# Linear attention, routed experts and a gated MLP on one core: sums and scales of the next expert at the step's end, y stored from ScalarE's queue, raw weights loaded one unit ahead

## The chip, the cores and the metric

One core of one Trainium2 chip runs the kernel. The metric is the device time of one execution in microseconds (us), here the median of three runs. TensorE (PE) does the matmuls, VectorE (DVE), ScalarE (ACT) and GpSimd (POOL) the elementwise work, SyncE (SP) issues most of the DMAs. Each of these engines carries out its own instructions in program order and waits on semaphores for the others.

## What is computed

Three stages follow each other (cut to what matters):

```python
# 1 linear attention, 8 batches x 8 heads x 576 tokens x 64
kv = einsum(softmax(k, over tokens), v);  x = softmax(q) @ kv      # x: 4608 x 512
# 2 routed experts, 8 of them, one per token
e = argmax(normalised(x) @ normalised(expert_emb).T / tau)
x = gate_w * (relu(x @ w1[e]) @ w2[e])                             # 512 -> 1024 -> 512
# 3 gated MLP
xn = x / rms(x) * rms_g
out = (silu(xn @ w_gate) * (xn @ w_val)) @ w_out                   # 512 -> 1536 -> 512
```

## The kernel before, in words

After the attention and the routing (up to about 188 us) the tokens are sorted by expert into blocks of 128, and the expert phase goes over them one block per **step** (`block(b, b0)`, from L1055). With these inputs 37 blocks hold tokens: steps 0 to 17 belong to one expert, 18 to 26 to the next, 27 to 31 and 32 to 36 to two more. All products are made of fp16 pieces: a high and a low half of each fp32 operand, three matmuls for one.

In step b PE runs the first product of block b (`g1_mm`, L1002: 96 matmuls of 128 columns from the transposed tokens `xT` and the weights `w1h`, `w1l`) and then the second product of block b-1 (`g2`, L1019: 24 matmuls of 512 columns from `hh`, `hl` and `w2h`, `w2l`). ACT evacuates the first product to `hh` (L1008) and DVE takes the remainder `hl` (L1009), both in two halves. ACT evacuates the second product of block b-1 to the tile `y` (`g2_ev`, L1026), scaled by a column `scl` that DVE made (L992); POOL writes the token's number into the last column of `y` (L1027) and SP stores the tile to `yscr` (L1028, 256.5 KB).

The weights of the next expert are made ready in the same steps by work that stands in conditional parts (`tc.If`), whose flags `r` and `rz` are read from a table at run time:

- last step of an expert (17, 26, 31): `split_stage(0, ...)` splits `w1` into halves (ACT L954, DVE L959), then SP loads the raw `w1` of the expert after it (`load_stage`, L898);
- first step of an expert (`rz` = 1: 18, 27, 32): `second_split` does the same for `w2` and loads the next (L901);
- third step (`rz` = 2: 2, 20, 29): `norm_parts`, six sums of squares on ACT (L913) and two maxima on DVE (L915) of the raw weights;
- fourth step (`rz` = 3: 3, 21, 30): `norm_scale`, a chain of small DVE instructions from L938 to L141 that makes the scale `wS` and its inverse `wI`.

`second_split`, `norm_parts` and `norm_scale` stand in one conditional part, `If(rz > 0)` at L1086, between the hidden activations and the evacuation of y. The instructions of PE's `g2` wait until ACT and DVE have left this part in the step before, since it can write `w2h` and `w2l`.

Beside this a filler (`fill`, three steps at L1085 and one at the end of the step) prepares the 36 weight tiles of the gated MLP: SP loads a `raw` tile (L1151, 512 KB), DVE turns it from float64 to float32 (L141, L142, L1181 to L1185), and later ACT (L1160) and DVE (L1161) split it. Three `raw` buffers are there and the load of unit k+2 is issued when unit k begins. From the end of step 31 on what is left of the filler is drained.

`prefetch(b)` at the start of a step has POOL gather the tokens of block b+3 and SP issue the transpose DMA of block b+2 into `xT` (L988, three buffers).

All DMAs of SP's and ACT's queues take turns on eight completion counters, DMAHW0 to DMAHW7 in the order listings below. A DMA is not issued before the one that had the counter before it has landed; a conditional part with DMAs in it that is passed over also moves its counters on, and waits in the same way.

From about 597 us the gated MLP runs to the end. Its matmuls follow each other almost without a gap.

Of the kernel before, what the change touches and what calls it, by code (L numbers as in the profile page):

```python
# [9 lines left out]
F32 = mybir.dt.float32  # L10
# [8 lines left out]
ET = mybir.EngineType  # L19
# [4 lines left out]
NT, DM = B * S, H * D  # L24
E, F = 8, 1024
FF = 1536
NTI = NT // 128
NBLK = NTI + E - 1
# [104 lines left out]
class Kern:  # L133
# [441 lines left out]
    def route_ops(self, s):  # L575
# [5 lines left out]
        for g in range(NTI // GT):  # L581
# [64 lines left out]
            for j in range(n):  # L646
                self.bd[i0 + j] = s.op(
                    ("V", 0.16), lambda j=j, i0=i0, bx=bx: self.ts(self.B[:, i0 + j, 0:129].rearrange("p (a c) -> p a c", c=3), self.io3[:, :, 0:3], bx["w"][:, j : j + 1], op0=ALU.is_equal),
                    [w], 0.05 if last else pr + 3, use=[T], late=last)
# [371 lines left out]
        self.yp[b] = p  # L1021

    def g2_ev(self, b):
        nc, p = self.nc, self.yp.pop(b)
        y = self.mp.tile([128, DM + 1], F32, tag="y", name=f"y{b}", bufs=3)
        nc.scalar.activation(y[:, 0:DM], p, AF.Copy, scale=self.scl.pop(b))  # L1026
        nc.gpsimd.tensor_copy(y[:, DM : DM + 1], self.tokf[:, b : b + 1])  # L1027
        nc.sync.dma_start(self.yscr[b * 128 : b * 128 + 128, :], y)  # L1028

    def reg(self, k, b, engines, mx=1):  # L1030
        return self.nc.values_load(self.flag[0:1, k, b : b + 1], engines=engines, min_val=0, max_val=mx)
# [23 lines left out]
    def block(self, b, b0):  # L1055


        tc = self.tc
        es = (ET.Activation, ET.DVE, ET.SP)
        r = self.reg(0, b, es, 4) if b + 1 < NBLK else None  # L1060
        rz = self.reg(1, b, es, 3)
        rx = [self.reg(2, k, (ET.SP,), E - 1) for k in (b, b + 1) if k < NBLK]
        self.h[b] = tuple(self.mp.tile([128, E, 128], F16, tag=t, name=f"{t}{b}", bufs=2) for t in ("hh", "hl"))
        p = [self.g1_mm(b, hf) for hf in range(2)]
        self.xT.pop(b)
        if b > b0:
            self.g2(b - 1)
        self.g1_ev(b, 0, p[0])
        if r is not None:
            with tc.If(r > 0):  # L1070
                with tc.If(r > 1):
                    if b > b0:
                        with tc.If(r > 3):
                            self.second_split(rx[0])
                    with tc.If(r > 2):
                        self.norm_parts()
                    self.norm_scale()
                self.split_stage(0, (0, 1))
        self.g1_ev(b, 1, p[1])
        if r is not None:  # L1080
            with tc.If(r > 0):
                self.split_stage(0, (2, 3))
                self.load_stage(rx[1], ("w1",))
        if b:
            self.fill(FILL[0])  # L1085
        with tc.If(rz > 0):  # L1086
            with tc.If(rz < 2) as c:
                if b > b0:
                    self.second_split(rx[0])
            with c.Else():  # L1090
                with tc.If(rz < 3) as c2:
                    self.norm_parts()
                with c2.Else():
                    self.norm_scale()
        self.scale_of(b)
        if b > b0:
            self.g2_ev(b - 1)
        if b:
            self.fill(FILL[1])

    def last(self, b):
        self.g2(b)
        if b + 1 < NBLK:
            r, rx = self.reg(0, b, (ET.Activation, ET.DVE, ET.SP), 4), self.reg(2, b + 1, (ET.SP,), E - 1)
            with self.tc.If(r > 0):
                self.second_split(rx)
        self.g2_ev(b)
# [4 lines left out]

    def experts(self, b0, b1):
        if b0 == 0:
            self.experts_start()
        for b in range(b0, b1):
            self.prefetch(b)
            self.block(b, 0)
        self.drain(self.filler)

    def tail(self):

        lv = self.reg(3, 0, (ET.PE, ET.Activation, ET.DVE, ET.SP, ET.Pool), NBLK)
        for b0, b1 in TAIL:
            with self.tc.If(lv > b0):
                for b in range(b0, b1):
                    if b > NTI:
                        self.gather(b)
                        self.gather_f(b)
                        self.transp(b)  # L1130
                    self.block(b, b0)
                self.last(b)


    def prep_units(self):

        nc, v, A = self.nc, self.nc.vector, self.A
        p = self.pp
        nc.scalar.dma_start(self.rms, A["rms"].rearrange("(c p) -> p c", p=128))
        order = [(m, u) for m in "gvo" for u in range(12)]  # L1140
        raws = {}

        def load(k):
            if k < len(order):
                m, u = order[k]
                if m == "o":
                    src = A["wo"][u * 128 : u * 128 + 128, :]
                else:
                    src = A["w" + m][(u // 3) * 128 : (u // 3) * 128 + 128, (u % 3) * 512 : (u % 3) * 512 + 512]
                t = p.tile([128, 512], mybir.dt.int64, tag="raw", name=f"raw{k}", bufs=3)  # L1150
                nc.sync.dma_start(t, src)  # L1151
                raws[k] = t

        def f32(k):
            return self.W[:, k + 1].rearrange("p a b -> p (a b)").bitcast(F32)

        def final(m, k0, sc):
            for j in range(12):
                w, c = k0 + j, sc if m == "o" else sc[:, j // 3 : j // 3 + 1]
                nc.scalar.activation(self.W[:, w, 0, :], f32(w), AF.Copy, scale=c)  # L1160
                v.scalar_tensor_tensor(self.W[:, w, 1, :], f32(w), c, self.W[:, w, 0, :], ALU.mult, ALU.subtract)  # L1161
                yield

        load(0)
        load(1)
        fin = iter(())
        yield
        yield from self.slot_steps()
        for k, (m, u) in enumerate(order):
            load(k + 2)  # L1170
            if u == 0:
                mx = p.tile([128, 12], F32, tag="mx", name=f"mx{m}")
            r = raws.pop(k).bitcast(I32).rearrange("p (n t) -> p n t", t=2)
            lo, hi = r[:, :, 0], r[:, :, 1]
            a = p.tile([128, 512], I32, tag="pa", name=f"pa{k}")
            c = p.tile([128, 512], I32, tag="pc", name=f"pc{k}")
            self.ts(a, hi, 0x7FFFFFFF, op0=ALU.bitwise_and)
            self.ts(c, hi, -0x80000000, 0x40000000, ALU.bitwise_and, ALU.bitwise_or)
            self.ts(a.bitcast(F32), a.bitcast(F32), HI_MIN, op0=ALU.max)
            yield  # L1180
            v.scalar_tensor_tensor(c, lo, 29, c, ALU.logical_shift_right, ALU.bitwise_xor)  # L1181
            self.ts(a, a, 3, 0x7FFFFFFF, ALU.logical_shift_left, ALU.bitwise_and)
            yield
            v.tensor_tensor(f32(k).bitcast(I32), a, c, ALU.bitwise_xor)
            v.tensor_reduce(mx[:, u : u + 1], f32(k), axis=AX.X, op=ALU.max, apply_absolute_value=True)  # L1185
            next(fin, None)
            yield
            if u == 11:
                fin = final(m, k - 11, self.w_scale(m, mx))
        for k, _ in enumerate(fin):  # L1190
            yield
            if k % 2:
                yield
# [446 lines left out]
```

## Time and profile before

| | |
|---|---|
| median of 3 runs | 1386.21 us (1385.81, 1386.21, 1386.93) |
| profiled execution | 1388.57 us |
| span of the profile in it | 1386.8 us |
| PE busy | 1337.3 us, 96% |
| DVE, ACT, POOL busy | 843.2, 577.7, 445.7 us |
| expert phase | from about 188 to 597 us |
| mean granted clock of TensorE | 0.985 |

The span is the part of the execution that the profile shows; 1.8 us of the profiled execution lie around it. A row of a timeline gives the start, the length, the engine, the line and operation, the tiles, and in brackets how long the engine had been idle before and what ended that.

### The profile page before, as it was taken

The page shows a single profiled execution, that of the slowest core. Times are in us where ns is not written, and L with a number is a line of the kernel's source. Part 1 is how long each engine was busy: PE and PEld are TensorE (multiplying, and loading weights), DVE is VectorE, ACT ScalarE, POOL GpSimd, SP SyncE. Part 2 cuts the span into 40 slices and gives each one's busy share as a digit, 9 for nine tenths or more (in the row PEclk, how much of TensorE's full clock was granted, in tenths as well). Part 3 has the DMA queues.
Part 4 walks back from the last instruction along what each step waited for, and adds up shares of the span by engine and source line. Part 5 has one row for each costly group of instructions (what it writes and reads, how often), then busy time and mean ns, then how long its engine had stood idle before and what let it go on. Part 6 is the DMA issues. An engine that isn't in the chain of part 4 may idle for free.

```text
span 1386.8 us, 29691 instructions
## 1 busy us (share of the span) xinstructions
PE 1337.3 (96%) x11415; PEld 984.3 (71%) x11415; DVE 843.2 (61%) x1842; ACT 577.7 (42%) x1104; POOL 445.7 (32%) x447
## 2 busy tenths in 40 slices
PE   8999679999998999999999999999999999999998
PEld 8988567777775766744486784867858678586783
DVE  5899877566797776257856363563535536355350
ACT  5888813112334356335543243342423424234231
POOL 4777652222222222043632222322132221322211
PEclk8999889999999999999999999999999999999999
DMA  8799376755596565520211303112031130402100
GB/s 296 268 295 304 109 225 144 147 154 137 136 244 154 161 164 145 133 57 0 70 45 31 84 2 80 35 37 79 2 84 32 41 75 1 91 25 47 39 1 31
DMA packets 151977, 145.78 MB, mean 105 GB/s; under 512 B 108901, under 2 KB 108937, under 8 KB 151761
## 3 DMA queue, kind: packets, MB, share of 16 engines
q1 hardware_dynamic: 141328, 114.64, 31.5%
q0 software_dynamic: 9904, 28.62, 6.9%
q8 instruction: 91, 1.49, 0.5%
q14 instruction: 126, 1.02, 0.3%
q10 hardware_dynamic: 528, 0.00, 0.0%
HBM read 87.35 MB, written 30.45 MB: 85 GB/s over the span
## 4 chain that ended last, share of the span: by engine, by line
PE 46%; DVE 5%; issue 3%; ACT 1%; DMA 1%; POOL 0%; POOLq 0%; DVEq 0%; ACTq 0%
PE po L1466 16%; PE pc L1382 9%; PE pa L1382 9%; PE pd L1382 9%; PE pb L1382 4%; DVE a L1336 1%; DVE xn L1298 1%; DVE ul L1457 1%; DVE hold L1354 1%; DVE u L1455 1%; DMA out<-o,tokr 1%; DVE S L1354 1%; ACT uh L1456 0%; DMA xnT<-xn 0%; POOL ul L1426 0%
## 5 line engine op out<-in xcount | busy, mean ns | idle before, releaser
L1466 PE MATMUL po<-W,uh 128*128 128x512 f16 x864 | 256.9, 379 | 0.0
L1382 PEld LDWEIGHTS <-W 128*128 128x128 f16 x2304 | 225.4, 98 | 28.8 <-issue 0.9
L1002 PE MATMUL hp<-xT,w1h 128*128 128x128 f16 x2368 | 205.4, 220 | 2.7 <-DMA xT<-xg 1.4
L1002 PE MATMUL hp<-xT,w1l 128*128 128x128 f16 x1184 | 203.0, 221 | 4.1 <-DVEq L1070 4.1
L1002 PEld LDWEIGHTS <-w1h 128*128 128x128 f16 x2368 | 185.3, 99 | 11.4 <-ACTq L1070 1.8
L1382 PEld LDWEIGHTS <-S 128*128 128x128 f16 x1728 | 169.1, 98 | 19.6
L1466 PE MATMUL po<-W,ul 128*128 128x512 f16 x432 | 163.7, 379 | 0.0
L1466 PEld LDWEIGHTS <-uh 128*128 128x128 f16 x864 | 84.5, 98 | 100.3
L1382 PE MATMUL pa<-xnT,W 128*128 128x256 f16 x1152 | 141.5, 273 | 0.5 <-ACT s L1391 0.5
L1002 PEld LDWEIGHTS <-w1l 128*128 128x128 f16 x1184 | 116.8, 99 | 4.7 <-DVEq L1070 4.6
L1019 PE MATMUL yp<-w2h,hh 128*128 128x512 f16 x296 | 112.1, 379 | 3.6 <-ACT wjunk L913 3.5
L1019 PE MATMUL yp<-w2l,hh 128*128 128x512 f16 x296 | 112.2, 379 | 2.6 <-DVE wI L141 2.4
L1394 DVE TENSOR_TENSOR u<-pb,s 128x512 f32<-128x512 f32 x48 | 33.2, 691 | 131.4 <-PE pb L1382 109.3
L1019 PEld LDWEIGHTS <-hh 128*128 128x128 f16 x592 | 56.4, 98 | 69.2 <-issue 8.9
L1009 DVE SCALAR_TENSOR_TENSOR hl<-hp,hh 128x512 f16<-128x512 f32 x74 | 51.1, 690 | 85.4 <-ACTq L1070 43.4
L1426 POOL TENSOR_TENSOR ul<-u,uh 128x512 f16<-128x512 f32 x32 | 37.0, 1156 | 184.5 <-ACT uh L1425 184.5
L1425 ACT ACTIVATE uh<-u 128x512 f16<-128x512 f32 x48 | 30.2, 630 | 145.9 <-DVE u L1423 145.9
L1008 ACT ACTIVATE hh<-hp 128x512 f16<-128x512 f32 x74 | 44.0, 595 | 111.9 <-PE hp L1002 102.1
L1471 POOL DMA_INDIRECT out<-o,tokr x36 | 37.1, 1030 | 160.7 <-ACT o L1470 160.6
L1466 PEld LDWEIGHTS <-ul 128*128 128x128 f16 x432 | 42.3, 98 | 51.0
L974 POOL DMA_INDIRECT xf<-fscr,tok x37 | 42.9, 1160 | 89.8 <-DVE scl L992 74.3
L1470 ACT ACTIVATE o<-po,co 128x512 f32<-128x512 f32 x36 | 24.7, 685 | 111.1 <-PE po L1466 111.1
(347 smaller groups left out, 2580.8 us busy)
## 6 DMA issues: line engine op xcount, KB each, us to landing
yscr<-y SPq DMA_DIRECT2D x37, 256.5 KB, 3.3
kt<-in_kT SPq DMA_DIRECT2D x16, 576.0 KB, 6.0
q<-in_q SPq DMA_DIRECT2D x12, 768.0 KB, 6.8
xscr<-row SPq DMA_DIRECT2D x36, 256.0 KB, 3.7
vt<-in_v SPq DMA_DIRECT2D x8, 1024.0 KB, 8.5
w1s<-in_w SPq DMA_DIRECT2D x8, 1024.0 KB, 7.2
w2s<-in_w SPq DMA_DIRECT2D x8, 1024.0 KB, 7.9
raw<-in_wg SPq DMA_DIRECT2D x12, 512.0 KB, 3.7
```

Of the source, the lines that this page charges most:

```text
L974: self.nc.gpsimd.indirect_dma_start(out=out, out_offset=None, in_=src, in_offset=bass.IndirectOffsetOnAxis(ap=self.tok[:, b : b + 1], axis=0),
L1002: nc.tensor.matmul(p[:, fc * 128 : fc * 128 + 128], w[:, dc, fs], xT[:, x, :], start=(fc == 0 and k == 0), stop=(fc == 3 and k == 11), ski ...
L1008: self.nc.scalar.activation(oh, p, AF.Relu)
L1009: self.nc.vector.scalar_tensor_tensor(ol, p, 0.0, oh, ALU.max, ALU.subtract)
L1019: nc.tensor.matmul(p, h[:, fc, :], w[:, fc, :], start=k == 0, stop=k == 23)
L1354: self.nc.vector.tensor_tensor(lo, t, hi, ALU.subtract)
L1382: nc.tensor.matmul(p[:, q * 256 : q * 256 + 256], self.left(k, self.m_, i, q, dcl, w), x[:, r, c : c + 256], start=first and n == 0, stop= ...
L1394: v.tensor_tensor(u2, b, s1, ALU.add)
L1425: nc.scalar.activation(uh[sl], uv, AF.Copy)
L1426: (v if i == 2 else nc.gpsimd).tensor_tensor(ul[sl], uv, uh[sl], ALU.subtract)
L1466: nc.tensor.matmul(p, t[:, fc, sl], self.W[:, 24 + fc, w, :], start=k == 0, stop=k == 35)
L1471: nc.gpsimd.indirect_dma_start(out=self.A["out"], out_offset=bass.IndirectOffsetOnAxis(ap=self.tokr[j][:, s : s + 1], axis=0), in_=o, in_o ...
```

## The change

1. `g2_ev` issues the store of `y` from ACT's queue, right behind ACT's evacuation, and no longer from SP's. The tile is allocated and POOL's copy of the token numbers made at the start of the step (`y_rows`).
2. `norm_parts` and `norm_scale` leave the conditional part ahead of the y evacuation and get one of their own at the step's end, `If(rz > 1)`, behind y and the last filler step. The part ahead keeps `second_split` alone, and is left out in step 0.
3. The load of a raw tile is issued one unit ahead (`load(k + 1)`) in place of two; the load of the second tile ahead of the phase goes.
4. The expert number of the next step is kept in a register (`self.rx`), which saves SP one register load per step.

```diff
     def g2_ev(self, b):
-        nc, p = self.nc, self.yp.pop(b)
-        y = self.mp.tile([128, DM + 1], F32, tag="y", name=f"y{b}", bufs=3)
+        nc, p, y = self.nc, self.yp.pop(b), self.y.pop(b)
         nc.scalar.activation(y[:, 0:DM], p, AF.Copy, scale=self.scl.pop(b))
-        nc.gpsimd.tensor_copy(y[:, DM : DM + 1], self.tokf[:, b : b + 1])
-        nc.sync.dma_start(self.yscr[b * 128 : b * 128 + 128, :], y)
+        nc.scalar.dma_start(self.yscr[b * 128 : b * 128 + 128, :], y)
+
+    def y_rows(self, b):
+        self.y[b] = self.mp.tile([128, DM + 1], F32, tag="y", name=f"y{b}", bufs=3)
+        self.nc.gpsimd.tensor_copy(self.y[b][:, DM : DM + 1], self.tokf[:, b : b + 1])
...
     def block(self, b, b0):
...
-        rx = [self.reg(2, k, (ET.SP,), E - 1) for k in (b, b + 1) if k < NBLK]
+        rx = [self.rx[k] if k in self.rx else self.reg(2, k, (ET.SP,), E - 1) for k in (b, b + 1) if k < NBLK]
+        self.rx = {b + 1: rx[-1]}
+        if b > b0:
+            self.y_rows(b - 1)
...
         if b:
             self.fill(FILL[0])
-        with tc.If(rz > 0):
-            with tc.If(rz < 2) as c:
-                if b > b0:
+        if b > b0:
+            with tc.If(rz > 0):
+                with tc.If(rz < 2):
                     self.second_split(rx[0])
-            with c.Else():
-                with tc.If(rz < 3) as c2:
-                    self.norm_parts()
-                with c2.Else():
-                    self.norm_scale()
         self.scale_of(b)
         if b > b0:
             self.g2_ev(b - 1)
         if b:
             self.fill(FILL[1])
+        with tc.If(rz > 1):
+            with tc.If(rz < 3) as c:
+                self.norm_parts()
+            with c.Else():
+                self.norm_scale()
...
     def prep_units(self):
...
         load(0)
-        load(1)
...
         for k, (m, u) in enumerate(order):
-            load(k + 2)
+            load(k + 1)
```

How the instructions stand, on ACT in step 20 (a step with `norm_parts`), before, from the last filler step to the first `hh` of step 21:

```order
L1160 ACTIVATE W<-W,rscv 128x512
L1086 COMPARE_AND_BRANCH
L1087 COMPARE_AND_BRANCH
L954 ACTIVATE w2h<-w2s,wS 128x1024 x4
L1087 UNCONDITIONAL_BRANCH
L1091 COMPARE_AND_BRANCH
L913 ACTIVATE wjunk,wq<-w1s 128x1024 x4
L913 ACTIVATE wjunk,wq<-w2s 128x1024 x2
L1091 UNCONDITIONAL_BRANCH x2
L1086 UNCONDITIONAL_BRANCH
L1026 ACTIVATE y_9262<-yp_9120,scl_8928 128x512
L1008 ACTIVATE hh_9322<-hp_0_9324 128x512
```

and in the change (y_8836 is the same tile, y of block 19):

```order
L1168 ACTIVATE W<-W,rscv 128x512
L1092 COMPARE_AND_BRANCH
L1093 COMPARE_AND_BRANCH
L954 ACTIVATE w2h<-w2s,wS 128x1024 x4
L1092 UNCONDITIONAL_BRANCH
L1025 ACTIVATE y_8836<-yp_8938,scl_8725 128x512
L1026 DMA yscr<-y_8836 128x513
L1100 COMPARE_AND_BRANCH
L1101 COMPARE_AND_BRANCH
L913 ACTIVATE wjunk,wq<-w1s 128x1024 x4
L913 ACTIVATE wjunk,wq<-w2s 128x1024 x2
L1008 ACTIVATE hh_9131<-hp_0_9133 128x512
```

The six sums (L913) now stand behind the y evacuation and behind ACT's own issue of the store, and ahead of the next `hh`.

On SP, the end of step 19 and the start of step 20, before, with what each waits for (raw_8872 and raw_8958 are units 25 and 26, y_8930 is y of block 18, xT_8974 the transposed tokens of block 22):

```order
L1151 DMA raw_8872<-in_wo 128x512 [waits DMAHW4_49,DVE_49]
L1086 COMPARE_AND_BRANCH
L1087 COMPARE_AND_BRANCH
L1087 UNCONDITIONAL_BRANCH
L1086 UNCONDITIONAL_BRANCH [waits DMAHW5_49,DMAHW6_49]
L1028 DMA yscr<-y_8930 128x513 [waits DMAHW7_49,Activation_49,Pool_49]
L1151 DMA raw_8958<-in_wo 128x512 [waits DMAHW2_49,DMAHW0_49,DVE_49]
L988 DMA_TRANSPOSE xT_8974<-xg_8634 128x8x128 [waits DMAHW1_49,DMASW4_49,PE_49]
```

and in the change (raw_8699 and raw_8753 are units 24 and 25, xT_8800 the tokens of block 22 again), with the store that now stands on ACT as the last row:

```order
L1159 DMA raw_8699<-in_wo 128x512 [waits DMAHW3_49,DVE_49]
L1092 COMPARE_AND_BRANCH
L1093 COMPARE_AND_BRANCH
L1092 UNCONDITIONAL_BRANCH [waits DMAHW4_49,DMAHW5_49]
L1159 DMA raw_8753<-in_wo 128x512 [waits DMAHW6_49,DMAHW1_49,DVE_49]
L988 DMA_TRANSPOSE xT_8800<-xg_8469 128x8x128 [waits DMAHW0_49,DMAHW4_49,DMASW4_49,PE_49]
L1026 DMA yscr<-y_8836 128x513 [waits DMAHW0_49,Activation_49,Pool_49]
```

Ahead of the transpose SP has no y store any more. The store of y of block 19 on ACT uses the counter DMAHW0, which the transpose of block 22 had just before it.

## Rows read from the trace of the kernel before

**Rows 1.** The page's busy time by engine (us, share of span, instructions), PE's part of it.
```profile
PE 1337.3 (96%) x11415; PEld 984.3 (71%) x11415; DVE 843.2 (61%) x1842; ACT 577.7 (42%) x1104; POOL 445.7 (32%) x447
```
**Rows 2.** Windows: stretch, its us, busy us of each engine, clock, DMA share, GB/s.
```profile
400.00:440.00 40.00, 35.29 (x412) 25.87 (x411) 33.05 (x92) 15.90 (x26) 9.02 (x11) 1.00 0.73 171
500.00:550.00 50.00, 46.57 (x531) 33.52 (x529) 33.48 (x82) 28.62 (x42) 7.29 (x9) 1.00 0.52 130
600.00:1387.00 787.00, 779.95 (x5605) 548.10 (x5603) 409.87 (x680) 287.90 (x557) 223.95 (x192) 1.00 0.17 41
```
**Rows 3.** Waits of PE, 180 to 600 us: in total, times, longest.
```profile
PE yp L1019 <- ACT wjunk L913: 3.5, 6, 2.7
PE yp L1019 <- DVE wI L141: 2.4, 2, 1.5
```
**Rows 4.** Timeline of PE, 405 to 440 us, the two longest waits.
```profile
418.89 0.38 PE L1019 MATMUL yp<-w2h,hh 128*128 128x512 f16 x1 [2.70 <-ACT wjunk L913]
...
432.30 0.38 PE L1019 MATMUL yp<-w2l,hh 128*128 128x512 f16 x1 [1.54 <-DVE wI L141]
```
**Rows 5.** Timeline of ACT: the same evacuation in two undisturbed steps one after the other.
```profile
255.51 0.60 ACT L1008 ACTIVATE hh<-hp 128x512 f16<-128x512 f32 x1 [1.69 <-PE hp L1002]
...
266.05 0.60 ACT L1008 ACTIVATE hh<-hp 128x512 f16<-128x512 f32 x1 [2.00 <-PE hp L1002]
```
**Rows 6.** Timeline of ACT, 405 to 428 us: first sum of step 20, and what follows them.
```profile
415.33 1.06 ACT L913 ACTIVATE wjunk<-w1s 128x1024 bf16<-128x1024 f32 x1 [5.80 <-SPq L1081]
...
422.29 0.67 ACT L1026 ACTIVATE y<-yp,scl 128x512 f32<-128x512 f32 x1
422.86 1.30 ACT L1008 ACTIVATE hh<-hp 128x512 f16<-128x512 f32 x2
```
**Rows 7.** Timeline of DVE: unit 25 begins; the scales of step 21, first instruction, and behind them.
```profile
414.60 0.42 DVE L141 TENSOR_SCALAR pa<-raw 128x512 int32<-128x512 int32 x1
...
429.09 0.16 DVE L938 TENSOR_TENSOR wq<-wq 128x2 f32<-128x2 f32 x1
...
432.68 0.16 DVE L992 TENSOR_TENSOR scl<-xf,comp 128x1 f32<-128x1 f32 x1
```
**Rows 8.** Timeline of SP's queue (issues), around steps 19 and 20.
```profile
397.70 3.86 SPq L988 DMA_TRANSPOSE xT<-xg  x1
...
409.16 0.33 SPq L1028 DMA_DIRECT2D yscr<-y  x1
...
410.07 1.26 SPq L988 DMA_TRANSPOSE xT<-xg  x1
```
**Rows 9.** Transpose, us from issue to landing: all 37; those issued at 397.70 and at 410.07.
```profile
DMA to landing us min/median/max: 3.4/5.8/11.4
...
xT<-xg SPq DMA_TRANSPOSE x1, 11.4
...
xT<-xg SPq DMA_TRANSPOSE x1, 7.3
```
**Rows 10.** Raw tile, us from issue to landing, all 36.
```profile
DMA to landing us min/median/max: 3.5/3.7/6.1
```
**Rows 11.** Waits of SP and DVE, 190 to 600 us: in total, times, longest.
```profile
SPq L1028 <- ACT y L1026: 89.0, 23, 8.0
SPq L1028 <- DMA xT<-xg: 3.2, 1, 3.2
DVE scl L992 <- DVEq L1086: 6.2, 25, 0.6
```
**Rows 12.** Timeline: the one DMA of this phase that ACT issues.
```profile
190.78 0.42 ACTq L1139 DMA_DIRECT2D rmsg<-in_rms  x1
```
**Rows 13.** Timeline of PE and ACT at the start of step 33, the last weights' split.
```profile
546.77 0.28 PE L1002 MATMUL hp<-xT,w1h 128*128 128x128 f16 x2 [1.28 <-ACTq L1070]
...
546.07 1.31 ACT L1008 ACTIVATE hh<-hp 128x512 f16<-128x512 f32 x2 [0.44 <-issue]
```
**Rows 14.** Timeline of PE at the end of the phase.
```profile
597.38 2.75 PE L1451 MATMUL pg<-xnT,W 128*128 128x512 f16 x12 [2.47 <-SPq L1105]
```

More of the change, by code (lines that the diff above doesn't have):

```diff
@@ L1099, in block @@
             self.fill(FILL[1])
+        with tc.If(rz > 1):
[3 more added lines that the diff above has]
+                self.norm_scale()
     def last(self, b):
+        self.y_rows(b)
         self.g2(b)
@@ L1114, in experts @@
         if b0 == 0:
+            self.rx, self.y = {}, {}
             self.experts_start()
@@ L1125, in tail @@
             with self.tc.If(lv > b0):
+                self.rx = {}
                 for b in range(b0, b1):
```

## The prediction, made before the change was run

> **What bounds the kernel now.** I read the page first: PE is busy for 1337.3 us, 96% of the span [rows 1], so only PE's idle time can be won. The windows by stretch say where it lies: from 600 us on PE is busy for 779.95 of 787 us and the clock is 1.00, while 400 to 440 us shows 35.29 of 40 and 500 to 550 us 46.57 of 50 [rows 2]. The change touches the expert phase alone, and what comes after 600 us moves as one piece. Then the waits of PE: its second product waits 3.5 us in six places for the sums (`wjunk`) and 2.4 us in two for the scales (`wI`) [rows 3]. This, 5.9 us, is all that moving those two parts can take away. PE's timeline puts most of it into two steps: 2.70 us at 418.89 and 1.54 us at 432.30 [rows 4], with three more of 0.16 us behind the first. I call these B (2.70 + 3 x 0.16 = 3.18) and C (1.54); what is left of the 5.9, about 1.2 us, lies in steps 30 and 31. In undisturbed steps PE waits for nothing: the same evacuation comes at 255.51 and 266.05, ended each time by PE [rows 5], which gives 10.54 us a step.
>
> **Why B is there.** ACT starts the sums of step 20 only at 415.33, after 5.80 us of waiting for SP, whose passage through the conditional parts of step 20 releases them [rows 6]. SP came late: it issued the transpose of block 22 at 410.07, just behind the y store at 409.16 [rows 8]. That store was held by the counter it shares with the transpose before, issued at 397.70, which took 11.4 us to land [rows 8, 9, 11]: 397.70 + 11.4 = 409.1. So the root of B is one slow transpose, and the sums' place only passes it on to PE.
>
> **Part 1, sums and scales at the step's end.** PE's g2 of step 21 wants to start at 418.89 - 2.70 = 416.2. It no longer waits for the sums, so B goes, and C with it: -4.7 us. But the sums are still 7 us of ACT (415.33 to 422.29) and everything queued behind them on ACT is late: `hh` of step 21, then DVE's `hl`, three filler steps, and the conditional part that PE's next g2 waits for. Before, DVE got there 429.09 - 415.33 = 13.8 us after the sums began [rows 6, 7]. Of this 0.6 us was the y evacuation (422.29 to 422.86), which now stands ahead of them; a further conditional part that is passed over costs DVE 6.2 / 25 = 0.25 us [rows 11]. That makes 13.4 us. PE wants that g2 at 416.2 + 10.54 = 426.7. With S the start of the sums, PE waits S + 13.4 - 426.7.
>
> What sets S now? ACT's y evacuation is done near 411.5, but the store behind it is ACT's own, and it shares its counter with the transpose of block 22: ACT stands there until that has landed. SP no longer has y stores ahead of its transposes, but the transpose of block 21 stays behind the `w2` load and comes only about 1 us sooner; raw unit 25 behind it shares its counter, so block 22's is issued near 408.6, some 1.5 us earlier than before. It lands 5.8 us (median) to 7.3 us (what this one took) later [rows 9]: S = 414.6 to 416.1 with 0.2 us for the passage. I take the middle, 415.4: PE waits 415.4 + 13.4 - 426.7 = 2.1 us. The scales (3.6 us of DVE, 429.09 to 432.68 [rows 7]) follow a step later; their wait lies between nothing and C's 1.5 us, and I take 0.3, because PE's own delay moves its need with it. So 2.4 of the 4.7 us come back in step 22. Bounds: 0 with S at 412, 5 and more with S above 418.
>
> A rule of the Trainium skill weighs on this part: DMA: Bandwidth & Descriptors, section "Issuing engines are not separate DMA queues", says that issuing on several engines saves only the sequencer's time to issue. The 89.0 us for which SP stood at the y stores [rows 11] speak for more than that, since it was the wait and not the issue; yet by the rule alone the transpose would stay at 410.07 and S at 417.6, and the sum would end 2 us higher, 1388.0, inside the forecast's own span below.
>
> **Part 2, steps 28 to 33.** Here ACT and DVE are the chain: PE starts the first product of block 33 at 546.77, after 1.28 us for ACT, whose `hh` came at 546.07 after only 0.44 us idle [rows 13]. The waits for sums and scales in steps 30 and 31 lie ahead of that one; taken away, they only lengthen it. So their 1.2 us count as nothing. Added to ACT's chain are three issues of y stores at 0.42 us [rows 12], 1.3 us, and three passed conditional parts at 0.25, 0.75 us. Without raw loads the counter of each store is that of the store a step before, long landed, so there is no wait. That is 2.0 us at most; 0.44 is idle that absorbs it, and I take +1.5. Bounds: -1.2, where the chain has room that I don't see, and +2.0.
>
> Advanced Engine Details and Errata of the Trainium skill, section "Control Flow Timing", gives about 0.108 us for a compare-and-branch; by an estimate from it the three parts would cost 0.3 and not 0.75 us, and the whole sum would be 0.4 us lower. The row of 0.25 us is the trace's own and decides.
>
> **Part 3, the end of the phase.** The last y stores and the first normalisations share ACT; PE waits there 2.47 us [rows 14] and one more issue of 0.42 us lies ahead of that: +0.4 (bounds 0 and +0.8).
>
> **Part 4, at nothing.** In undisturbed steps the y store on ACT costs 0.42 us of an engine that waits 1.7 to 2.0 us for PE each time [rows 5]; without this cover each step would be 0.4 us longer. POOL's copy keeps its place between the gathers. The raw load one unit ahead leaves about a step, 10.5 us, for a transfer of 3.7 us (6.1 at most [rows 10]). Unit 25 is the narrow one: issued near 408, needed by DVE at 414.60 [rows 7]; 408 + 6.1 = 414.1 just holds. SP's saved register load and the first step's missing part save time where nobody waits.
>
> **Sum.** -4.7 + 2.4 + 1.5 + 0.4 = -0.4 us. The profiled execution would go from 1388.57 to 1388.2 us; it lies 2.4 us above the median of the three runs, and I carry the difference over to the median: 1386.21 - 0.4 = 1385.8 us. About 0.2%, 2.8 us, is what a measurement of this kernel can tell from no change.
>
> **Rivals.**
>
> 1. *The waits go and do not come back.* The transpose of block 22 lands by 412 or the conditional parts are passed earlier than I count; then -4.7 stands, and steps 28 to 33 cost between -1.2 and +1.0. With +0.4 for the end: -3.3 to -5.5 in all, 1380.7 to 1382.9 us, say 1381.8. For it: the quickest transposes land in 3.4 us [rows 9] and SP is free of 89.0 us of waits. Against it: around step 20 they took 7.3 and 11.4 us.
> 2. *ACT stands at the y store.* The wait that held SP, which nobody behind it needed at once, now holds ACT, and `hh` behind it is what PE needs. Place: the store of y of block 19 behind the transpose of block 22. Price: every microsecond that S lies after 413.3 is one of PE's, and at S = 418.6 the sum reaches +2.8. If it takes 11.4 us as the one before it did, S = 420.2, PE waits 7.2 us with the scales, and the sum is -4.7 + 7.2 + 1.5 + 0.4 = +4.4: 1390.6 us. For it: the 11.4 us; against it: the next took 7.3, with the weights' load over. DMA: Bandwidth & Descriptors of the Trainium skill, section "Anatomy of one DMA", says that a DMA's semaphore wait happens on the issuing sequencer ahead of dispatch. The trace agrees: SP stood 89.0 us at L1028.
> 3. *A raw unit lands late.* DVE's chain to the conditional part then waits for unit 25 or 26; each microsecond is PE's in step 22. Landing 2 us after 414.6 gives +1.6: 1387.8 us; 6 us, against every row, +5.6.
>
> **How the numbers follow.** The forecast, within 0.2%, has 0.46; rival 1 has 0.29, rival 2 0.20, rival 3 0.05, which I split between no change and slower. Hence faster 0.29, same 0.48, slower 0.23. The likeliest case itself spans 1383.7 (S at 413.3 or before, all else as taken) to 1388.8 (S = 418.4). For 8 in 10 the range reaches well into both sides: from 1381.4, most of rival 1, to 1389.4, the milder half of rival 2.
>
> **What would show it.** Right: ACT's first sum of step 20 stands behind the y evacuation near 415.4, PE's waits for `wjunk` and `wI` are gone from the list, and a new one of some 2 us stands near 429 at g2 of step 22, named by the conditional part of `second_split`; SP's wait for y is gone; PE's wait at the first product of block 33 has grown beyond 1.28 us. Wrong: no wait near 429 (rival 1), one of over 5 us there with ACT's queue held at the store (rival 2), DVE waiting for `raw` (rival 3), or a wait of PE in steps 4 to 17, which none of these has.

## The result and the profile after

The change is **slower by 0.5%**: the median is 1390.34 us (1387.20 to 1397.18, 14 runs) beside 1383.33 us (1379.23 to 1388.30, 14 runs) of the kernel before on the same chip, ratio 1.0051 with a 95% interval of 1.0034 to 1.0069. That is 7.0 us. The forecast, 1385.8 us and most likely no change, was wrong, and the time lies above the range. The profiled execution took 1390.85 us.

The page after, its span and busy line, and the windows of [rows 2] up to the MLP:

```profile
span 1389.1 us, 29723 instructions
...
PE 1335.3 (96%) x11415; PEld 980.9 (71%) x11415; DVE 845.5 (61%) x1842; ACT 579.1 (42%) x1104; POOL 441.9 (32%) x447
```
```profile
400.00:440.00 40.00, 36.78 (x420) 26.72 (x418) 33.03 (x92) 17.35 (x28) 9.81 (x13) 1.00 0.75 182
500.00:550.00 50.00, 44.29 (x471) 31.53 (x469) 31.66 (x79) 27.53 (x41) 6.81 (x8) 0.97 0.39 101
```

DVE and ACT are busy 2.3 and 1.4 us longer than before and PE 2.0 us less [rows 1], so it is PE's idle time that has grown. The first stretch, where B and C were, is fuller (36.78 us against 35.29); the second, where the forecast expected +1.5, is emptier (44.29 against 46.57). Its granted clock is 0.97 and not the 1.00 of [rows 2]. The two stretches below, of the change and then of before, show where: right after PE had waited 1.53 us at 522.42 the clock stood at 0.50, the lower of its two levels (1.2 of 2.4 GHz), and PE did 33 matmuls where it did 61 before. That is about 1.6 us lost, by an estimate from the 3.2 us of the row.

```profile
524.20:527.40 3.20, 3.20 (x33) 3.20 (x31) 1.82 (x5) 1.41 (x2) 0.00 (x0) 0.50 0.00 0
524.20:527.40 3.20, 3.20 (x61) 3.20 (x59) 2.17 (x9) 2.01 (x3) 0.00 (x0) 1.00 0.01 3
```

PE's waits from 185 to 610 us, which answer to [rows 3], and SP's line that answers to [rows 11]:

```profile
PE hp L1002 <- DVEq L1075: 10.4, 9, 2.1
PE hp L1002 <- ACTq L1075: 3.3, 3, 1.5
PE yp L1019 <- ACTq L1075: 1.7, 1, 1.7
PE yp L1019 <- DVE w2l L959: 0.7, 4, 0.2
```
```profile
SPq L1092 <- SPq L1092: 77.1, 21, 6.2
```

`wjunk` and `wI` are gone, as is SP's wait for y; SP now stands 77.1 us at the part at L1092 instead, since passing it over waits for the DMAs that had its counters. In place of `wjunk` and `wI`, PE's *first* product waits, in twelve places, for DVE or ACT to pass L1075: the conditional part that may write `w1h` and `w1l`, which stands between the two halves of `hh` and `hl`. Before, that cost 5.4 us in four places. PE's timeline puts the new waits there:

```profile
397.27 0.23 PE L1002 MATMUL hp<-xT,w1l 128*128 128x128 f16 x1 [1.26 <-DVEq L1075]
...
409.39 0.23 PE L1002 MATMUL hp<-xT,w1l 128*128 128x128 f16 x1 [1.41 <-DVEq L1075]
...
432.45 0.23 PE L1002 MATMUL hp<-xT,w1l 128*128 128x128 f16 x1 [1.81 <-DVEq L1075]
...
522.42 0.28 PE L1002 MATMUL hp<-xT,w1h 128*128 128x128 f16 x2 [1.53 <-ACTq L1075]
...
592.41 0.39 PE L1019 MATMUL yp<-w2h,hh 128*128 128x512 f16 x1 [1.74 <-ACTq L1075]
```

They lie in the first matmuls of steps 20, 21, 23 and 31 and in the last product. The starts of the steps on PE (the first matmul of each first product) give a table by stage, the yardstick of all that follows. Steps 19 to 23 hold one expert's sums and scales and steps 28 to 32 the next one's; "last" is the last step with its own second product.

| kernel | ratio, 95% interval | 19-23 | 28-32 | 33 | last |
|---|---|---|---|---|---|
| before | 1 | 58.21 | 56.82 | 11.18 | 10.70 |
| the change | 1.0051 [1.0034, 1.0069] | 58.95 | 62.45 | 11.38 | 12.62 |
| e1 raw only | 0.9986 [0.9971, 1.0000] | 58.84 | 57.95 | 11.18 | 10.70 |
| e2 parts only | 1.0027 [1.0013, 1.0040] | 57.04 | 61.65 | 11.18 | 10.70 |
| e3 y from ACT, tile early, register | 1.0001 [0.9985, 1.0017] | 55.45 | 57.01 | 11.40 | 12.89 |
| e4 as e3, y from SP | 0.9987 [0.9969, 1.0004] | 54.48 | 56.06 | 11.29 | 10.75 |
| e5 before + empty part | 1.0050 [1.0033, 1.0068] | 58.12 | 61.32 | 12.67 | 14.39 |
| e6 change, parts back | 1.0019 [1.0006, 1.0033] | 58.73 | 59.00 | 13.00 | 12.42 |
| e7 change, raw back | 1.0016 [1.0003, 1.0028] | 55.86 | 60.76 | 15.65 | 12.38 |
| e8 change, y from SP | 1.0032 [1.0017, 1.0047] | 56.40 | 60.86 | 11.52 | 12.47 |
| e9 the change again | 1.0062 [1.0038, 1.0085] | 60.94 | 60.99 | 14.03 | 12.80 |
| e10 e5, flags early | 1.0060 [1.0040, 1.0079] | 58.63 | 59.68 | 15.97 | 10.98 |
| e11 change, flags early | 1.0078 [1.0060, 1.0097] | 58.26 | 61.34 | 15.60 | 12.62 |
| e12 e4, flags early | 1.0055 [1.0035, 1.0075] | 56.10 | 59.58 | 18.07 | 12.00 |
| e13 e5, flags covered | 1.0029 [1.0008, 1.0050] | 56.01 | 57.83 | 14.42 | 16.24 |
| e14 change, flags covered | 1.0053 [1.0036, 1.0070] | 56.26 | 60.88 | 17.13 | 12.51 |
| e15 e4, flags covered | 1.0027 [1.0006, 1.0049] | 54.72 | 57.18 | 15.97 | 12.08 |
| e16 e4 again | 0.9978 [0.9958, 0.9998] | 57.16 | 55.82 | 11.73 | 14.20 |
| e17 e15 + parts moved | 1.0014 [1.0001, 1.0027] | 53.88 | 57.39 | 18.85 | 11.23 |

From the start of step 2 to the MLP the change takes 395.35 us and before 386.97, 8.4 us more: +5.6 in steps 28 to 32 (about 1.6 of it the lower clock), +1.9 in the last step, +0.7 in 19 to 23, and +0.1 in all the rest. Steps 0 and 1 took 1.2 us less, and the MLP is 789.4 us in both. The spans still differ by only 2.3 us, because the attention and the routing, which the change does not touch, took 4.9 us less in this profile (183.1 us up to the first expert product, before 188.0); over the profiles of all kernels that part varies from 182.1 to 188.0 us. So the 7.0 us of the medians can't be read from one pair of profiles.

Each ratio is against runs of the kernel before on the same chip. Its median was 1384.47 us where e1 to e4 ran and between 1392.9 and 1395.4 us on the three chips of the later runs. Those show step 33 and the last step changing from run to run (e4 and e16 are one kernel, 10.75 and 14.20), and no profile of before stands beside them there, so comparisons between chips go by steps 19 to 23 and 28 to 32. Two profiles of one kernel differ there by up to 2.7 and 1.5 us (the change and e9, e4 and e16); a single difference below that is no more than a hint. Three entries hold a stretch at the lower clock, worth about 1.6 us each by the same estimate: 28 to 32 of the change and of e11, and 19 to 23 of e6.

### The profile page after: what moved, and what is told of

Its sections match the earlier page's. It is cut to its first block, busy times and chain, and to the rows that moved or that the text cites. A ratio compares the mean times of both kernels' runs of the same rounds, so it can differ in the third digit from the quotient of the medians.

```text
span 1389.1 us, 29723 instructions
## 1 busy us (share of the span) xinstructions
PE 1335.3 (96%) x11415; PEld 980.9 (71%) x11415; DVE 845.5 (61%) x1842; ACT 579.1 (42%) x1104; POOL 441.9 (32%) x447
## 4 chain that ended last, share of the span: by engine, by line
PE 52%; issue 3%; DVE 1%; DMA 1%; POOL 0%; ACT 0%; POOLq 0%; DVEq 0%
PE po L1473 18%; PE pc L1389 9%; PE pa L1389 8%; PE pd L1389 8%; PE pb L1389 4%; PE pv L1458 2%; PE pg L1458 2%; DMA out<-o,tokr 1%; DVE c L1430 0%; POOL ul L1433 0%; DVE c L1441 0%; ACT uh L1432 0%; POOLq L1643 0%; DVE u L1430 0%; DVE u L1404 0%
```

## The experiments

### Each part alone

**Raw one ahead, on the kernel before** (e1). Edit:

```diff
         load(0)
-        load(1)
...
-            load(k + 2)
+            load(k + 1)
```

> Only the raw loads one unit ahead; all else as before. Measure: the time from PE's first expert matmul to the first matmul of the gated MLP, 409.4 us before and 416.6 with the whole change. Theory 1 (the loss is a sum of three parts): DVE waits some 2 to 2.6 us for a raw tile in steps 18 and 27, where the load stands behind the 2 MB load of w1, and PE gets 1.5 to 3 us of it: 411 to 412.5 us. Theory 2 (the stores on ACT make the loss): 409.4, no wait that counts. Theory 3 (the further conditional part makes it): 409.4.

Measured: 0.9986, nothing lost. But DVE's timeline shows the raw unit late, in step 18:

```profile
385.74 0.43 DVE L141 TENSOR_SCALAR pa<-raw 128x512 int32<-128x512 int32 x1 [3.49 <-SPq L1081]
```

This is the third rival at another place: the load is issued on SP right behind the 2 MB of `w1` that the end of step 17 fetches, and lands late. In the time of e1 that costs nothing.

**The parts at the step's end, on the kernel before** (e2): only the edit of `block` from the change.

> Only sums and scales in a conditional part at the step's end; y from SP and raw loads two ahead as before. Theory 1: the waits of 3.2 and 1.5 us around 419 and 432 go, but PE waits about 1.8 us for the conditional part ahead of the second half of hl after the scales' step, and 2 to 3 us more in steps 28 to 33: 408 to 411 us. Theory 2: only the gain is left, 404.5 to 406. Theory 3: the part costs 0.9 us ahead of hl in every step in which DVE has no slack: 412 to 416.

Measured: 1.0027, more than half of the loss. From PE's first expert matmul to the MLP it takes 412.7 us, as the third theory said. Steps 19 to 23 gain 1.2 us, which is within the spread, and steps 28 to 32 lose 4.8. DVE's timeline at the start of step 19, where the new part is only passed over:

```profile
395.32 0.69 DVE L1009 SCALAR_TENSOR_TENSOR hl<-hp,hh 128x512 f16<-128x512 f32 x1 [2.15 <-ACTq L1095]
```

**y on ACT's queue, with the early tile and the kept register** (e3), and **the same with the store left on SP** (e4). Against the change e3 puts `block`'s parts and the raw loads back; e4 differs from e3 by one word:

```diff
-        nc.scalar.dma_start(self.yscr[b * 128 : b * 128 + 128, :], y)
+        nc.sync.dma_start(self.yscr[b * 128 : b * 128 + 128, :], y)
```

> Only y from ACT's queue (and the register kept); sums and scales and raw loads as before. Theory 1: 0.4 to 0.8 us more of ACT in steps 28 to 36, where ACT is the chain: 410.5 to 412. Theory 2: ACT stands at the store behind a transpose in steps 19 to 21 and sums and hidden activations are late behind it: 414 to 417. Theory 3: 409.4.

> y tile and token numbers at the step's start and the register kept, but y stored from SP, sums and scales and raw loads as before. Every theory: as before within 0.5 us, 409 to 410; another value would mean that POOL's order or SP's register loads carry part of it.

Measured: 1.0001 and 0.9987, and 405.6 and 402.5 us from the first expert matmul to the MLP, less than any theory gave. The store's queue is worth nothing in the steps. The last step of e3 takes 2.19 us more than the 10.70 of before, with ACT idle for 2.40 us behind its own store; what stands in such a gap is shown further down.

In e4's profile B and C are smaller without any part being moved. PE's timeline:

```profile
409.70 0.38 PE L1019 MATMUL yp<-w2l,hh 128*128 128x512 f16 x1 [0.65 <-DVE wq L915]
...
421.21 0.38 PE L1019 MATMUL yp<-w2l,hh 128*128 128x512 f16 x1 [0.81 <-DVE wI L141]
```

The transpose of block 22 is issued 6.5 us after the start of step 20 (399.31 against 392.77); before it was 9.9 us (410.07 [rows 8] against 400.13). But this does not hold for the kernel: in e16, which is e4 again, it is issued after 9.2 us, and B and C are nearly what they were, as PE's timeline of e16 shows:

```profile
419.81 0.38 PE L1019 MATMUL yp<-w2h,hh 128*128 128x512 f16 x1 [1.65 <-ACT wjunk L913]
...
433.21 0.38 PE L1019 MATMUL yp<-w2l,hh 128*128 128x512 f16 x1 [1.53 <-DVE wI L141]
```

In the eleven profiles with the sums and scales in their old place, PE's waits for them in steps 21 and 22 come to between 1.2 and 4.7 us, and the 4.7 of before is the largest. So B and C vary from run to run, and what makes e4 a little faster stays open.

### What the new conditional part costs

**A conditional part that is never taken, on the kernel before** (e5). Nothing is moved; the flag is at most 3, so the part never runs:

```diff
-        rz = self.reg(1, b, es, 3)
+        rz = self.reg(1, b, es, 4)
...
             self.fill(FILL[1])
+        with tc.If(rz > 3):
+            self.norm_parts()
+            self.norm_scale()
```

> The kernel before with one more conditional part at the step's end, which is never taken (sums and scales for a flag that no step has); nothing else moves. Measure: from the start of step 2 to the gated MLP, 387.0 us before, 395.4 with the change, 391.2 with sums and scales alone. Theory 1a (passing the part over costs more than 0.25 us: the engine finishes its own work first, and then fetches the next step's flags with nothing to cover it): DVE idle 0.9 us ahead of hl in steps 19, 20 and 28 to 33, and 389.5 to 392. Rival 1b (what costs is the work put in front of hh and hl, the part itself is hidden): 386.5 to 387.5.

Measured: 1.0050 beside the change's 1.0051. Passing the part by alone costs as much as the whole change lost. From the start of step 2 to the MLP it takes 395.9 us, more than the 389.5 to 392 that were expected; steps 28 to 32 take 61.32, 4.5 more than before. DVE's timelines at the same place of step 28, first of before, then of e5:

```profile
497.65 0.74 DVE L1161 SCALAR_TENSOR_TENSOR W<-W,rscv 128x512 f16<-128x512 f32 x1
498.31 0.68 DVE L1009 SCALAR_TENSOR_TENSOR hl<-hp,hh 128x512 f16<-128x512 f32 x1
```
```profile
501.42 0.74 DVE L1164 SCALAR_TENSOR_TENSOR W<-W,rscv 128x512 f16<-128x512 f32 x1
503.77 0.69 DVE L1009 SCALAR_TENSOR_TENSOR hl<-hp,hh 128x512 f16<-128x512 f32 x1 [1.61 <-ACTq L1086]
```

Before, `hl` follows the filler at once; with the part between them DVE stands for 1.61 us (the label names ACT's queue, which had passed 0.8 us earlier). ACT's timeline at the start of step 19 shows half of that:

```profile
397.39 0.71 ACT L1163 ACTIVATE W<-W,rscg 128x512 f16<-128x512 f32 x1
398.90 1.31 ACT L1008 ACTIVATE hh<-hp 128x512 f16<-128x512 f32 x2 [0.80 <-PE yp L1019]
```

Over steps 28 to 32 DVE's idle time ahead of `hl` is 2.13 us in before, 5.20 in e5 and 8.01 in the change, and ACT's ahead of `hh` 0.98, 3.96 and 3.93. Of the change's 8.01, one gap of 4.42 is another thing: there DVE waits for ACT behind the six sums. It stands in the same place in every kernel with the parts moved. DVE's timeline of the change:

```profile
522.35 0.69 DVE L1009 SCALAR_TENSOR_TENSOR hl<-hp,hh 128x512 f16<-128x512 f32 x1 [4.42 <-ACTq L1075]
```

In e5 each passing leaves DVE idle for 0.91 to 1.61 us and ACT for 0.79 to 1.18. Why so much more than the 0.25 us of [rows 11]? DVE's instructions from the filler to the next `hl`, before (into step 30) and in e5 (into step 31):

```
before  L1161 SCALAR_TENSOR_TENSOR W<-W,msco 128x512 [waits Activation_49]
        L1031 TENSOR_LOAD flag x2
        L1009 SCALAR_TENSOR_TENSOR hl_12068<-hp_0_12069,hh_12067 128x512 [waits Activation_49]
e5      L1100 UNCONDITIONAL_BRANCH [waits DVE_49]
        L1031 TENSOR_LOAD flag x2
        L1009 SCALAR_TENSOR_TENSOR hl_13289<-hp_0_13290,hh_13288 128x512 [waits Activation_49]
```

Behind the filler the next step reads its two flags, and before, that reading is hidden by the arithmetic still running. The way past the part ends in a wait for DVE's own instructions, so the flags are read only when DVE stands empty. The trace has these two loads (number, then shortest, median and longest in ns, then the first and the last start). At the place of step 28 above, first of before, then of e5:

```profile
L1031 DVEq TENSOR_LOAD <-flag x2: 299/306/314, 497.1 to 497.5; - x2
L1031 DVEq TENSOR_LOAD <-flag x2: 580/653/726, 502.3 to 502.9; - x2
```

Before, both run while DVE still reduces and splits. In e5 they begin when the filler has ended, and their 0.58 and 0.73 us make 1.31 of the 1.61 us. The passed parts of [rows 11] lie in mid-step with no reading behind them.

**The change with one part back** (e6: sums and scales back in the old place; e7: raw loads two ahead; e8: y from SP).

> The change with sums and scales put back into the one conditional part ahead of y. Theory 1 (sum of parts): what raw loads one ahead and the stores on ACT cost without it, 385.5 to 389 us. Rival (the parts only hurt together): as with sums and scales, 391 or more.

> The change with raw loads two units ahead again. Theory 1: no wait of DVE for raw in steps 18 and 27, the rest stays: 392 to 394 us. Rival (raw loads carry nothing, since they fit before): 395 to 396.

> The change with y stored from SP again (tile and token numbers still at the step's start). Theory 1: the tail's 2 us and ACT's waits of 2 us at two stores go: 391.5 to 393.5 us. Rival 2 (the stores on ACT make most of the loss): 386 to 388.

Measured: 1.0019, 1.0016 and 1.0032 against 1.0051 and 1.0062 of the change. Parts or raw loads taken back win clearly; y's gain is within the noise. The three gains add up to more than the loss, which fits costs that overlap. e6's 392.4 us from step 2 to the MLP is what its rival said, that the parts only hurt together. e6 wins in steps 28 to 32 (59.00), e7 and e8 in 19 to 23 (55.86 and 56.40): e7 is 2.4 us below before there, a hint by the spread above. There the late raw unit shows in the change, on DVE's timeline of it and in the time from issue to landing of this load (issued at 376.15):

```profile
386.49 0.43 DVE L141 TENSOR_SCALAR pa<-raw 128x512 int32<-128x512 int32 x1 [2.63 <-SPq L1086]
DMA to landing us min/median/max: 10.3/10.3/10.3
```

and is gone in e7. What cost nothing in e1 seems to cost some 3 us in 19 to 23 beside the rest of the change (e7 to the change +3.1, and +5.1 to e9; e3 to e6 +3.3, half of it the lower clock). These are single profiles from different chips.

### Is it the flags?

**The change again** (e9), and **the next step's flags read earlier**. In e10 (of e5), e11 (of the change) and e12 (of e4) they are read just ahead of the three filler steps, in e13, e14 and e15 just behind them:

```diff
+        if b + 1 < self.bend:
+            self.fl[b + 1] = self.flags(b + 1)
         if b:
             self.fill(FILL[0])
```

> The change as it is, on the chip on which the next three run. All theories: from the start of step 2 to the gated MLP 395.4 us within 2, as in its first profile.

> The kernel before with the never-taken part at the step's end, and the two flags of the next step fetched in the middle of the step, ahead of the filler. Theory 1a (the fetch of the flags behind the passed part is what costs): DVE's idle time ahead of hl in steps 19 and 28 falls from 1.0 and 1.6 us to 0.2 to 0.4, ACT's ahead of hh from 0.8 to 0.2; 387 to 389 us. Rival 1c (the jump itself costs, the engine's drained pipeline and the fetch of instructions behind it): 0.8 to 1.6 stays, 392 to 396.

> The change with the flags fetched in the middle of the step. Theory 1a: four to five us less than the change, 390.5 to 392; what is left is ACT's waits at two stores, a late raw tile in steps 18 and 27 and the last step. Rival 1c: 394 to 396.

> The kernel with tile and token numbers of y at the step's start and the register kept (383.2 us, e4), with the flags fetched in the middle of the step and no further part. Theory 1a: at the passing of the one part ahead of y the fetch is hidden by the filler, so 382 to 384; rival 1c: the same. It is there to see whether the early fetch alone gains.

Measured: the change again loses 0.6%, and takes 398.5 us from step 2 to the MLP, 1.1 beyond the expected range. e10, e11 and e12 brought no gain: 1.0060, 1.0078, and e12 (1.0055) is worse than e4. DVE's idle time ahead of `hl` did fall, in e10 to 1.12 us over steps 28 to 32, but the place is just behind another passed part, that of the `w1` split, and the loss moved there: DVE's timeline of e12, where the two loads (0.93 and 0.31 us) fill most of the gap.

```profile
505.36 0.43 DVE L141 TENSOR_SCALAR pa<-raw 128x512 int32<-128x512 int32 x1 [1.54 <-SPq L1089]
```

So the place was badly chosen, and these three could not decide. The next three read the flags where DVE and ACT have filler work to run meanwhile.

> The never-taken part at the step's end (e5), with the next step's flags fetched behind the three filler steps, where DVE has work queued. Measures: steps 28 to 32 on PE (56.8 us before, 61.3 with the part, 59.7 with the fetch behind the split's part) and the last step (10.7, 14.4, 11.0). Theory 1a: 57 to 58 and 10.7 to 11. Rival 1c: 60 or more.

> The change with the fetch behind the filler. Steps 28 to 32 took 62.5 and 61.0 us with the change. Theory 1a: 58 to 59.5, and about 3 us less in all than the change. Rival 1c: 60.5 or more.

> Tile and token numbers of y early and the register kept (e4), with the fetch behind the filler, no further part. Steps 28 to 32 took 56.1 us with e4 and 59.6 with the fetch behind the split's part. Theory 1a: 55.5 to 57. Rival 1c says nothing on it.

> The kernel of e4 a second time, beside the kernel before: all theories: 0 to 4 us faster than before, mostly in steps 20 to 22, where SP comes to its conditional parts earlier by a register load a step.

Measured: with the empty part still there, steps 28 to 32 fall from 61.32 us (e5) to 57.83 (e13), within 1.0 of before. DVE's and ACT's timelines of e13 at the part:

```profile
503.01 0.74 DVE L1171 SCALAR_TENSOR_TENSOR W<-W,rscv 128x512 f16<-128x512 f32 x1
503.90 0.69 DVE L1009 SCALAR_TENSOR_TENSOR hl<-hp,hh 128x512 f16<-128x512 f32 x1 [0.15 <-DVEq L1105]
```
```profile
499.04 0.71 ACT L1170 ACTIVATE W<-W,rscv 128x512 f16<-128x512 f32 x1
499.86 1.31 ACT L1008 ACTIVATE hh<-hp 128x512 f16<-128x512 f32 x2
```

The part itself leaves DVE idle for 0.15 us, and the rest of the 1.61 goes with the loads. That settles what the passing costs in steps 28 to 32 of e5. The whole time shows it less well: 1.0029 against 1.0050, with intervals that overlap, and the last step took 16.24 us where 10.7 to 11 were expected. Nor does it mend the change. e14 wins in steps 19 to 23 (56.26 against 60.94 of e9 on the same chip), but takes 60.88 us in steps 28 to 32 (e9 60.99), as the rival of its expectation said. There DVE waits for a raw unit, and PE for ACT behind the sums; DVE's and PE's timelines of e14:

```profile
495.19 0.43 DVE L141 TENSOR_SCALAR pa<-raw 128x512 int32<-128x512 int32 x1 [2.94 <-SPq L1089]
...
529.05 0.29 PE L1002 MATMUL hp<-xT,w1h 128*128 128x128 f16 x2 [1.69 <-ACTq L1078]
```

Reading the flags early is not free either: e15 is 1.0027 where the same kernel without it is 0.9987 and 0.9978 (e4, e16). In the profiles step 33 is longer in all kernels with early flags, 14.42 to 18.85 us, but also in e7 (15.65) and e9 (14.03) without them. Two things stand in it: PE's first product waits between single matmuls for nothing that the profile shows (1.8 to 3.2 us in all with early flags), and in all of these but e13 the clock then falls to 0.50. In e12:

```profile
558.80:565.40 6.60, 5.33 (x43) 4.49 (x43) 2.51 (x5) 1.77 (x5) 2.46 (x4) 0.50 0.93 303
```

What starts these waits stays open.

**The parts moved, the flags covered, raw two ahead and y from SP** (e17; e15 with the change's edit of `block`).

> As e15 (tile and token numbers of y early, register kept, flags fetched behind the filler), with sums and scales in a part of their own at the step's end; y from SP, raw loads two ahead. e15: steps 19 to 23 54.7 us, steps 28 to 32 57.2. If the place of the taken parts costs by itself: 28 to 32 in 59 or more, and 19 to 23 in 53 to 55, since nothing is taken away there but the waits for sums and scales. If only passing the part cost: 56 to 57.5 and 51 to 53.5, faster than e15.

Measured: steps 19 to 23 53.88 us and 28 to 32 57.39, against 54.72 and 57.18 of e15. With the reading covered, moving the sums and scales costs nothing in 28 to 32, and wins less in 19 to 23 than the 51 to 53.5 us that were expected. What e14 has beyond e17, the raw load one ahead and y on ACT, is worth 2.4 and 3.5 us in the two stretches. So the change's loss in 28 to 32 has two causes, and each alone holds it near 61 us: the uncovered loads (e5, e2) and, beside the moved parts, this pair (e14). Which of the pair does it was not tried. The ratio, 1.0014, is still no gain over before. The one version with a sign of beating both kernels, by 0.1 to 0.2%, is **e4's**: 0.9978 with an interval below 1 in e16, 0.9987 with an interval that just holds 1 in e4.

## Why the prediction was wrong

- **B and C go: right, but -4.7 was too much.** No wait for `wjunk` or `wI` is left. B's 3.2 of the 4.7 us came from one slow transpose, as the forecast itself found; in the ten other profiles with the parts in their old place these waits are 1.2 to 3.7 us. That e7 gains 2.4 us in steps 19 to 23, beside the forecast's -4.7 + 2.4 = -2.3, is in part luck, since the wait that came back stands elsewhere.
- **S: right in its place, and the second rival small.** That the measured 1390.34 us is close to this rival's 1390.6 is chance. ACT's timeline of the change at the end of step 20:

```profile
407.91 0.69 ACT L1025 ACTIVATE y<-yp,scl 128x512 f32<-128x512 f32 x1 [0.48 <-PE yp L1019]
410.26 0.34 ACTq L1026 DMA_DIRECT2D yscr<-y  x1
410.91 1.06 ACT L913 ACTIVATE wjunk<-w1s 128x1024 bf16<-128x1024 f32 x1 [2.31 <-DVEq L1086]
```

  The sums start 15.2 us after the start of step 20 (395.73); the forecast's 415.4 lies 15.3 us after that of before (400.13). ACT stood at the store for 410.26 - 408.60 = 1.66 us here, until the transpose of block 22 had landed, 7.0 us after its issue at 403.14. A step earlier it stood for 1.96 us, until SP had passed the part at L1075 over; in all other steps but the first it was 0.08. The rule of the Trainium skill, DMA: Bandwidth & Descriptors, "Anatomy of one DMA", that the wait happens on the issuing sequencer, agrees with these two.
- **Where the 2.4 comes back: wrong place.** Nothing waits near 429 at the second product. DVE's late `hl` holds back the part at L1075 first, so PE waits at the first product of step 23 (1.81 us at 432.45), behind the scales and two flag loads, for which the forecast had 0.3. The 1.26 and 1.41 us in steps 20 and 21 have no term in it.
- **The step that failed: "a further conditional part that is passed over costs DVE 6.2 / 25 = 0.25 us".** The row was of parts in mid-step. At the step's end a passed part left DVE idle for 0.91 to 1.61 us and ACT for 0.79 to 1.18 in e5, because the two flag loads behind it run uncovered. In part 2, three times 0.25 was part of +1.5 for steps 28 to 33; measured in 28 to 32 were +4.5 in e5, where nothing else is new, +4.8 in e2 and +5.6 in the change (+4.2 in e9, without the fall of the clock). In the whole change this is not the only cause, as e14 shows. In steps without sums and scales it had been put at nothing, and that held: steps 2 to 18 took 179.61 us against 179.18, and the 0.43 lies in step 5, behind the scales.
- **Raw one ahead at nothing: wrong in the change, right alone.** The third rival looked at unit 25; the late ones were needed at 386.49 and 486.94, behind the loads of `w1` at the end of steps 17 and 26. The forecast took 6.1 us for the longest transfer; behind the `w1` loads it took 10.3.
- **The end, +0.4: mis-sized.** The last step costs +1.9 (and +2.2 in e3), less 0.55 for the start of the MLP. The store costs not its issue of 0.34 us alone but the gap behind it on ACT's timeline of the change (0.66 us at the same place of before). Three register loads stand in this gap, 0.28, 0.58 and 0.56 us: ACT's queue first waits at the store for the end of y, so they begin only then, while before they begin under the evacuation of y. It is the same mechanism as at the passed part. Kernels with y from SP reach 12 us and more there too on the later chips (e8, e15, e16), so the +1.9 itself is no more than a hint.

```profile
589.67 0.34 ACTq L1026 DMA_DIRECT2D yscr<-y  x1
591.75 1.31 ACT L1008 ACTIVATE hh<-hp 128x512 f16<-128x512 f32 x2 [2.16 <-issue]
...
L1033 ACTq TENSOR_LOAD <-flag x3: 281/562/576, 590.0 to 591.1; - x3
```

- **SP's queues.** The rule of the Trainium skill weighed in the forecast, DMA: Bandwidth & Descriptors, "Issuing engines are not separate DMA queues", by which only issue time is saved, is borne out by e3 against e4: 1.0001 and 0.9987, no gain from the second queue, though SP's 89.0 us of waits for y are gone; in e3 SP stands at its raw loads instead, 57.7 us for DVE. "SP's saved register load ... save time where nobody waits" may be the other miss: with the early tile (e4, e16) it is the one part of the change with a sign of gain, 0.1 to 0.2%.

## What to carry to other kernels

Price a conditional part by what stands behind it: passed over in mid-step it cost 0.25 us here, but ahead of register loads that arithmetic used to hide it cost 0.8 to 1.6 us on each engine. A DMA issue that waits for the engine's own result uncovers such loads in the same way. Test such a part empty before moving work into it. And take a change of several parts apart: here the raw loads alone were harmless and seemed to cost time beside the rest, and undoing any one part left a loss.

## What the runs showed of the chip that was not expected

- A register load of a flag took 0.31 us on DVE and 0.28 on ACT (medians over the phase in e5), and single ones up to 1.0. Two of them, uncovered, make most of the 0.91 to 1.61 us of a passed part in e5, far more than the branch: covered, 0.15 us is left in e13. Advanced Engine Details and Errata of the Trainium skill, "Control Flow Timing", gives about 0.108 us for a compare-and-branch; the 0.15 us of the part alone is near that size, and the 1.61 is not.
- On the chips of the later runs PE's first product in steps 0 and 1 waits 4.5 to 6.3 us in all, in 5 to 12 places between single matmuls, with no releaser but "issue"; on the first chips the list of waits shows none there. PE's timeline of e5:

```profile
200.96 0.22 PE L1002 MATMUL hp<-xT,w1h 128*128 128x128 f16 x1 [0.99 <-issue]
...
203.92 0.26 PE L1002 MATMUL hp<-xT,w1h 128*128 128x128 f16 x1 [0.82 <-issue]
```

  In e5 the clock fell behind these waits: it is 1.00 from 195 to 202.2 us and 0.50 from 202.4 to 209. Over steps 0 and 1 the mean granted clock is 0.72 to 0.83 in the later runs and 0.84 to 0.91 in the first, and the two steps take 28.5 to 30.5 us and 19.4 to 22.5. That is of the size of the 8 to 12 us by which the kernel before is slower on the later chips, though no profile of it was taken there. What holds the instructions back was not tried.
